# Four ordering edges in a one-core transformer block: two on VectorE and two normalisations on ScalarE

## The chip, the cores and the metric

The kernel runs on one NeuronCore of a Trainium2 chip. The metric is device time in microseconds (us) of one execution. PE is TensorE, DVE is VectorE, ACT is ScalarE, SP is the engine that issues most of the DMAs (307 of 325 in the kernel before). The profile's span (first to last instruction) is about 1.8 us shorter than the timed value of the same execution. Each execution also comes with a mean granted TensorE clock, 1.000 being full speed.

## The reference, cut to what matters

```python
phi = lambda t: jnp.where(t > 0, t + 1, jnp.exp(t)) + 1e-6
q, k, v = split(layernorm(x) @ wqkv)                    # S = 2048, D = 1024, 32 heads of 32
kv = einsum("bhsd,bhse->bhde", phi(k), v);  z = sum over s of phi(k)
o = (phi(q) @ kv) / (phi(q) . z + 1e-6)
h = x + o @ wo
h2 = h + ((relu(hn @ W_gate)) * (hn @ W_up)) @ W_down   # hn = layernorm(h), F = 3584
```

## The kernel before

Every large product is one level of Strassen-like block products: seven products in place of eight, with sums of operand blocks made beforehand on VectorE and partial results copied out of PSUM, the memory that TensorE adds its products up in, between the products; to copy a PSUM bank out is to evict it (0.68 us for one of 128x512 on VectorE in the second K unit). Three stages matter here.

*K units.* Each takes four token tiles; the first of the four units is computed plainly, the others start near 39, 67 and 95 us. (This text counts them from one; the prediction counts from zero, so its K unit 1 is the second here.) In the last three `strassen` accumulates products in the PSUM banks A, D and E. ScalarE copies the accumulators out (`snap`), VectorE evicts D and E (`phi_begin`), and both also normalise x for later units or make operand sums for the next product.

```python
def right_ops(w, t):                        # operand sums of a weight, on VectorE
    def sums():
        tensor_tensor(out=t1, in0=b12, in1=b11, op=subtract)
        tensor_tensor(out=t2, in0=b22, in1=t1, op=subtract)
        tensor_tensor(out=t3, in0=b22, in1=b12, op=subtract)   # in the place of b12
        tensor_tensor(out=t4, in0=b21, in1=t2, op=subtract)

def phi_begin(dst, ps, m):                  # evicts a PSUM bank
    if m is None: nc.scalar.activation(out=dst, in_=ps[:], func=Identity, bias=..., scale=1.0)
    else:         nc.vector.scalar_tensor_tensor(out=dst, in0=ps[:], scalar=1.0 + PHI_EPS, in1=m, ...)

def phi_end(dst, e):
    nc.scalar.activation(out=e, in_=dst, func=Exp, ...)
    nc.vector.tensor_scalar(out=e, in0=e, scalar1=1.0, scalar2=PHI_EPS, op0=min, op1=add)   # "the clip"
    nc.vector.tensor_tensor(out=dst, in0=dst, in1=e, op=max)
```

*The attention tail (200 to 232 us).* For each token tile: `nd` matmuls (numerator and denominator), the division on VectorE (`o_sb`), a DMA transpose, 16 `attn` matmuls with wo, an addition of the residual on VectorE (`x_res`), a normalisation on ScalarE (`hn`), and a DMA transpose of `hn`.

*The first quad of the gated layer* starts in the middle of that. Its operands are sums of the transposed `hn` and of the gate and up weights, all on VectorE:

```python
def left_sums(T, S, cols, eng):             # for each token tile of the second half of a group
    eng.tensor_tensor(out=s1, in0=a21, in1=a22, op=add)        # "hs", reads the transposed hn
    eng.tensor_tensor(out=s2, in0=s1, in1=a11, op=subtract)
    eng.tensor_tensor(out=a21, in0=a11, in1=a21, op=subtract)
    eng.tensor_tensor(out=s4, in0=a12, in1=s2, op=subtract)
...                                          # then weight sums: "tg", "tu"
```

A list scheduler decides the order of the instructions on each engine from a model of their durations. An edge "behind" orders two instructions of one engine and adds no wait; but everything else on that engine, and on others, may then be placed anew.

## Time and profile before

| | kernel before |
|---|---|
| time, first 6 runs | 738.26 us median (737.57 to 739.62) |
| time, 33 runs beside the experiments | 738.47 us median, 738.68 mean |
| span of the profiled run | 737.2 us, clock 1.000 |
| PE busy | 98% of the span |

PE is the bound; the gain to be had is in the 14.5 us that it idles (737.2 - 722.7). A line of the order of time reads: start, duration, engine, source line, operation, output<-input, shapes, count, and in brackets the idle time before it and what ended that. Source lines shift by up to a dozen between the kernels (`o_sb` is L534 before and L544 after); go by the tile names.

### The profile page before, as it was taken

The page shows a single profiled execution, that of the slowest core. Times are in us where ns is not written, and L with a number is a line of the kernel's source. Part 1 is how long each engine was busy: PE and PEld are TensorE (multiplying, and loading weights), DVE is VectorE, ACT ScalarE, POOL GpSimd, SP SyncE. Part 2 cuts the span into 40 slices and gives each one's busy share as a digit, 9 for nine tenths or more (in the row PEclk, how much of TensorE's full clock was granted, in tenths as well). Part 3 has the DMA queues.
Part 4 walks back from the last instruction along what each step waited for, and adds up shares of the span by engine and source line. Part 5 has one row for each costly group of instructions (what it writes and reads, how often), then busy time and mean ns, then how long its engine had stood idle before and what let it go on. Part 6 is the DMA issues. An engine that isn't in the chain of part 4 may idle for free.

```text
span 737.2 us, 10549 instructions
## 1 busy us (share of the span) xinstructions
PE 722.7 (98%) x3967; PEld 381.8 (52%) x4020; DVE 556.0 (75%) x980; ACT 321.5 (44%) x580; POOL 20.7 (3%) x56
## 2 busy tenths in 40 slices
PE   8999999999989999999999999999999999999997
PEld 3444555444444444444444444444444458888667
DVE  6997644676789767688768787887786479996677
ACT  4776553778786655444344444443444120000000
POOL 0000000000000000000000000000000001100210
PEclk9999999999999999999999999999999999999999
DMA  9765002079977526175638358575483499978932
GB/s 315 169 145 157 0 1 95 21 168 230 215 166 166 135 73 208 43 207 135 196 106 243 114 188 270 182 219 193 162 280 120 137 392 343 305 253 283 257 44 58
DMA packets 143811, 128.88 MB, mean 175 GB/s; under 512 B 50960, under 2 KB 126096, under 8 KB 143760
## 3 DMA queue, kind: packets, MB, share of 16 engines
q1 hardware_dynamic: 136688, 123.30, 55.6%
q0 software_dynamic: 5312, 3.15, 3.4%
q10 hardware_dynamic: 1760, 1.77, 0.7%
q8 instruction: 31, 0.51, 0.3%
q14 instruction: 20, 0.16, 0.1%
HBM read 76.81 MB, written 39.85 MB: 158 GB/s over the span
## 4 chain that ended last, share of the span: by engine, by line
PE 85%; DVE 7%; DMA 4%; ACT 3%; issue 1%; SPq 0%; DVEq 0%; POOL 0%; ACTq 0%
PE accA L832 22%; PE accX L832 8%; PE accY L832 8%; PE accA L1167 8%; PE attn L557 6%; PE Aq L733 4%; PE Aq L314 3%; PE accA L993 3%; PE accX L1167 3%; PE Aq L454 3%; PE accY L1167 2%; PE Eq L314 2%; PE accY L993 2%; PE accX L993 2%; PE Eq L733 2%; DVE stats L272 1%
## 5 line engine op out<-in xcount | busy, mean ns | idle before, releaser
L842 ACT ACTIVATE gu<-gu 128x512 bf16<-128x512 bf16 x72 | 45.4, 630 | 131.3 <-DVE gu L841 131.3
L837 ACT COPY snap<-accA 128x1024 f32<-128x1024 f32 x72 | 72.5, 1008 | 36.5 <-PE accA L832 36.4
L832 PEld LDWEIGHTS <-tg 128*128 128x128 f16 x384 | 37.6, 98 | 45.3
L832 PEld LDWEIGHTS <-tu 128*128 128x128 f16 x384 | 37.6, 98 | 45.3
L557 PE MATMUL attn<-wo_mem,oT 128*128 128x512 bf16 x247 | 57.9, 379 | 2.6 <-DVE o_sb L534 1.3
L841 DVE TENSOR_TENSOR gu<-accY,snap 128x1024 bf16<-128x1024 f32 x36 | 43.9, 1219 | 10.0 <-ACT snap L837 10.0
L832 PE MATMUL accA<-hn,tg 128*128 128x512 f16 (+1 forms) x192 | 49.3, 379 | 0.0
L832 PE MATMUL accA<-hn,tu 128*128 128x512 f16 (+1 forms) x192 | 49.3, 379 | 0.0
L841 DVE TENSOR_TENSOR gu<-accX,snap 128x1024 bf16<-128x1024 f32 x36 | 43.9, 1219 | 6.4 <-PE accX L832 3.7
L154 ACT COPY u<-Aq 128x512 f32<-128x512 f32 x54 | 31.3, 581 | 36.6 <-PE Aq L314 19.3
L1167 PEld LDWEIGHTS <-x 128*128 128x128 f16 (+1 forms) x448 | 43.9, 98 | 5.5
L832 PEld LDWEIGHTS <-wu 128*128 128x128 bf16 x288 | 28.2, 98 | 34.0
L832 PEld LDWEIGHTS <-wg 128*128 128x128 bf16 x288 | 28.2, 98 | 34.0
L557 PEld LDWEIGHTS <-oT 128*128 128x128 bf16 x256 | 24.6, 98 | 32.5 <-issue 4.1
L845 DVE TENSOR_TENSOR hq<-gu 128x512 bf16<-128x512 bf16 x48 | 20.3, 423 | 14.3 <-ACT gu L842 14.2
L314 PEld LDWEIGHTS <-xT 128*128 128x128 bf16 (+1 forms) x192 | 18.6, 98 | 23.6 <-issue 2.3
L534 DVE TENSOR_TENSOR o_sb<-nd,rd 128x384 bf16<-128x384 f32 (+1 forms) x48 | 23.4, 508 | 8.3 <-ACT rd L533 6.1
L1131 POOL DMA_DIRECT2D out_dram<-o x12 | 15.2, 1265 | 508.8 <-DMA h<-h_dram 419.1
L1167 PEld LDWEIGHTS <-xs 128*128 128x128 f16 x280 | 27.4, 98 | 3.2
L560 DVE SCALAR_TENSOR_TENSOR x_res<-attn,x_res 128x512 bf16<-128x512 f32 x32 | 22.0, 686 | 8.6 <-PE attn L557 8.5
L1173 DVE TENSOR_TENSOR snap<-accA,u 128x1024 f32<-128x1024 f32 x16 | 19.5, 1221 | 11.4 <-PE accA L1167 11.3
L993 PEld LDWEIGHTS <-x 128*128 128x128 bf16 (+1 forms) x168 | 16.4, 98 | 19.6
(235 smaller groups left out, 1420.3 us busy)
## 6 DMA issues: line engine op xcount, KB each, us to landing
x<-x_dram SPq DMA_DIRECT2D x17, 896.0 KB, 8.8
x_dram<-hq SPq DMA_DIRECT2D x28, 512.0 KB, 3.2
wg<-in_B_W_gate_dram SPq DMA_DIRECT2D x14, 512.0 KB, 5.1
wu<-in_B_W_up_dram SPq DMA_DIRECT2D x14, 512.0 KB, 7.3
wraw<-in_B_W_down_dram SPq DMA_DIRECT2D x14, 512.0 KB, 4.9
x_dram<-hq SPq DMA_DIRECT2D x28, 256.0 KB, 2.7
t_dram<-wt SPq DMA_DIRECT2D x28, 256.0 KB, 2.2
xd<-x_dram SPq DMA_DIRECT2D x6, 896.0 KB, 6.9
```

The source lines that it names most:

```text
L154: copies[nm, v] = nc.scalar.copy(out=snaps[nm, v], in_=bank[v][:])
L314: nc.tensor.matmul(ps[:], lhsT=left[m - 1][:, kc, r + v * P:r + (v + 1) * P], rhs=right[m - 1][:, kc, :], start=(start and kc == 0), stop= ...
L454: nc.tensor.matmul(ps[:], lhsT=rq[m - 1][:, kc, (c + v) * P:(c + v + 1) * P], rhs=left[m - 1][:, kc, :], start=(start and kc == 0), stop=( ...
L534: nc.vector.tensor_tensor(out=ov[:, c0:c0 + n], in0=ndv[:, :, 0:P].rearrange("p k (h e) -> p k h e", h=HPC), in1=rd[:, 0:n, :].unsqueeze(3 ...
L557: nc.tensor.matmul(ps[:], lhsT=st["oT"][:, c, :], rhs=wo_sb[:, c, j * NW:(j + 1) * NW], start=(c == 0), stop=(c == KC - 1))
L733: nc.tensor.matmul(ps[:], lhsT=w(v, m)[:, kc, :], rhs=left[m - 1][:, kc, :], start=(start and kc == 0), stop=(kc == KH - 1), skip_group_ch ...
L832: nc.tensor.matmul(ps[:, v, :], lhsT=w[v][n - 1][:, kc, :], rhs=left[n - 1][:, kc, :], start=(t is not None and kc == 0), stop=(kc == KH - ...
L837: nc.scalar.copy(out=st[nm][:], in_=halves(st["A"]))
L841: add(out=g[:], in0=halves(st[nm]), in1=st[base][:], op=ALU.add)
L842: nc.scalar.activation(out=g[:, 0, :], in_=g[:, 0, :], func=ACT.Relu)
L993: nc.tensor.matmul(ps[:, t * NW:(t + 1) * NW], lhsT=x_tile(n, s, kh)[:, f, (t0 + t) * P:(t0 + t + 1) * P], rhs=w_tile(n, kh)[:, f, :], sta ...
L1167: nc.tensor.matmul(pv[:, tt, :], lhsT=left(m)[:, f, tt * P:(tt + 1) * P], rhs=right(m)[:, f, :], start=(t is not None and f == 0 and tt % ...
```

## The change

The intent is to take away five short waits of PE, by order alone. Part A: two normalisations of x go behind accumulator copies of the second K unit on ScalarE. Part B: the second q sum goes behind the first D eviction of the fourth and last K unit, near 97 us, and so no longer stands ahead of the third's. Part C: the last clip of the q side goes behind the `x_res` addition of a tile. No arithmetic changes.

```diff
+    def behind(late, first):
+        tc.add_manual_dep(late.ins, first.ins.name, <order only, same engine>)
+    normed, k_copies, k_begins, q_ends = {}, {}, {}, {}
 ...   (the instructions concerned are kept in these dictionaries)
-        q_sums()
+        behind(q_sums(), k_begins[NU - 1, 0, 0, 0])                              # part B
+        for t, copy in ((atiles[10], ("m1", 1)), (atiles[11], ("u3", 0))):
+            behind(normed[t], k_copies[1][copy])                                 # part A
 ...
     with tc.issue_after(added[order[STS], 0].ins):
         late_sums.pop()()
+    behind(q_ends[NS - 1, KH - 2, 1, 0], added[order[STS], 0])                   # part C
```

(`q_sums()` returns its second instruction; two older edges were only rewritten with `behind`. So the new edges are four.)

More of the change, by code (lines that the diff above doesn't have):

```diff
@@ L133, in sums @@
             nc.vector.tensor_tensor(out=t1, in0=b12, in1=b11, op=ALU.subtract)
-            nc.vector.tensor_tensor(out=t2, in0=b22, in1=t1, op=ALU.subtract)
+            second = nc.vector.tensor_tensor(out=t2, in0=b22, in1=t1, op=ALU.subtract)
             nc.vector.tensor_tensor(out=t3, in0=b22, in1=b12, op=ALU.subtract)
             nc.vector.tensor_tensor(out=t4, in0=b21, in1=t2, op=ALU.subtract)
+            return second
         return (b11, b21, b22, t4, t1, t2, t3), sums
@@ L208, in phi_begin @@
         if m is None:
-            nc.scalar.activation(out=dst, in_=ps[:], func=ACT.Identity, bias=negb[:, 1:2], scale=1.0)
-        else:
-            nc.vector.scalar_tensor_tensor(out=dst, in0=ps[:], scalar=1.0 + PHI_EPS, in1=m,
-                                           op0=ALU.add, op1=ALU.add)
+            return nc.scalar.activation(out=dst, in_=ps[:], func=ACT.Identity, bias=negb[:, 1:2], scale=1.0)
+        return nc.vector.scalar_tensor_tensor(out=dst, in0=ps[:], scalar=1.0 + PHI_EPS, in1=m,
+                                              op0=ALU.add, op1=ALU.add)
     def phi_end(dst, e):
         nc.scalar.activation(out=e, in_=dst, func=ACT.Exp, bias=negb[:, 0:1], scale=1.0)
-        nc.vector.tensor_scalar(out=e, in0=e, scalar1=1.0, scalar2=PHI_EPS, op0=ALU.min, op1=ALU.add)
+        clipped = nc.vector.tensor_scalar(out=e, in0=e, scalar1=1.0, scalar2=PHI_EPS, op0=ALU.min, op1=ALU.add)
         nc.vector.tensor_tensor(out=dst, in0=dst, in1=e, op=ALU.max)
+        return clipped
+    def behind(late, first):
+        tc.add_manual_dep(late.ins, first.ins.name,
+                          mybir.DependencyInfo(mybir.DependencyClass.NoSync, mybir.DependencyReason.DATA),
+                          reason="order")
+    normed, k_copies, k_begins, q_ends = {}, {}, {}, {}
     order = [(i * HS + s * SW) // P + tt for s in range(NS) for i in range(2) for tt in range(NT)]
@@ L287, in ln_T @@
             nc.vector.scalar_tensor_tensor(out=nmr, in0=mv[:, 0:1], scalar=-1.0, in1=rstd, op0=ALU.mult, op1=ALU.mult)
-            nc.scalar.activation(out=xn[:], in_=x_sb[:], func=ACT.Identity, bias=nmr, scale=rstd)
+            normed[t] = nc.scalar.activation(out=xn[:], in_=x_sb[:], func=ACT.Identity, bias=nmr, scale=rstd)
             if t not in atiles[:PE_T]:
@@ L305, in block_kernel, with token_unit @@
         pk, vs = {}, {}
-        def token_unit(u, right, fin):
+        def token_unit(u, right, fin, copies={}):
             s, _, r = place(units[u][0])
@@ L316, in mm @@
                                      stop=(kc == KH - 1), skip_group_check=True)
-            return strassen(pspool, awork, mm, fin)
+            return strassen(pspool, awork, mm, fin, 3, False, copies)
         def new_pk(t):
@@ L330, in fin @@
                     new_pk(t)
-                phi_begin(pk[t][:, j * NW:(j + 1) * NW], ps, m)
+                k_begins[u, i, j, v] = phi_begin(pk[t][:, j * NW:(j + 1) * NW], ps, m)
                 ready[t] = ready.get(t, 0) + 1
@@ L335, in fin @@
                     phi_end(pk[t], e[:])
-            return token_unit(u, rk, fin)
+            return token_unit(u, rk, fin, k_copies.setdefault(u, {}))
         def k_plain(t):
@@ L462, in fin @@
                 e = qw[-1].tile([P, 2, NW], BF16, tag="e", name="e")
-                phi_end(pair, e[:])
+                q_ends[s, c, i, j] = phi_end(pair, e[:])
         return strassen(pspool, qw[-1], mm, fin, 3, s == NS - 1 and c + 2 == KH)
@@ L790, in block_kernel @@
     for t, copy in ((order[-2], ("m1", 1)), (order[-1], ("u3", 1))):
-        tc.add_manual_dep(squared[t].ins, quad_copies[2][copy].ins.name,
-                          mybir.DependencyInfo(mybir.DependencyClass.NoSync, mybir.DependencyReason.DATA),
-                          reason="order")
+        behind(squared[t], quad_copies[2][copy])
     pqctx.close()
```

## The prediction

> **What bounds the kernel now.** I read the page's busy shares first, then PE's waits, then the order of time around each wait. PE is busy almost throughout:
>
> ```profile
> PE 722.7 (98%) x3967; PEld 381.8 (52%) x4020; DVE 556.0 (75%) x980; ACT 321.5 (44%) x580; POOL 20.7 (3%) x56
> ```
>
> The span is 737.2 us, so PE idles 14.5 us. Busy time by stretches puts 2.9 of it in the first 10 us, 3.7 after PE's last matmul, 1.7 between 39 and 82, 2.0 between 200 and 232, and 4.2 in all the rest. Nothing that moves work on DVE (VectorE) or ACT (ScalarE) can win more than the few waits in between. PE's waits name the ones that the change aims at:
>
> ```profile
> PE attn L557 <- DVE x_res L560: 0.8, 1, 0.8
> PE nd L527 <- DVE o_sb L534: 0.5, 1, 0.5
> PE Dq L314 <- DVE wo_mem L211: 0.5, 1, 0.5
> PE Aq L314 <- ACT m L154: 0.5, 1, 0.5
> PE Aq L314 <- ACT u L154: 0.3, 1, 0.3
> ```
>
> That view counts from a matmul's modelled end. I count from where the next could have started: eight 512-column matmuls take 1.73 us from start to start, so 0.216 each, and a 132-column one 0.058. By that the waits in the order of time, in their order here, are 0.98, 0.64, 0.64, 0.62 and 0.44 us. Outside these two stretches PE runs nearly without gaps and nothing is waiting to absorb a shift: what is lost or won at these places reaches the end undiminished.
>
> The order of time around the first two, DVE, PE and the DMA queue together:
>
> ```profile
> 210.93 0.43 DVE L217 TENSOR_SCALAR e<-e 128x1024 bf16<-128x1024 bf16 x1 [0.94 <-ACT e L216]
> 211.28 0.69 DVE L560 SCALAR_TENSOR_TENSOR x_res<-attn,x_res 128x512 bf16<-128x512 f32 x1
> ...
> 212.02 0.59 PE L557 MATMUL attn<-wo_mem,oT 128*128 128x512 bf16 x2 [0.82 <-DVE x_res L560]
> ...
> 213.02 1.23 SPq L581 DMA_TRANSPOSE hn<-hn  x1
> ...
> 216.07 0.96 DVE L534 TENSOR_TENSOR o_sb<-nd,rd 128x384 bf16<-128x384 f32 x2
> 216.94 0.68 DVE L560 SCALAR_TENSOR_TENSOR x_res<-attn,x_res 128x512 bf16<-128x512 f32 x1
> ...
> 217.55 0.42 DVE L117 TENSOR_TENSOR hs<-hn 128x512 f16<-128x512 bf16 x1
> ```
>
> The reader is to see three things. At 210.93 DVE had idled 0.94 us for an exponential while the x_res addition behind it was ready. The hn transpose is issued at 213.02. The first sum that reads it, hs on L117, runs at 217.55 without a wait, because two o_sb and one x_res stand ahead of it.
>
> The transpose of hn in that stretch, alone:
>
> ```profile
> DMA to landing us min/median/max: 4.4/4.4/4.4
> ```
>
> It lands at 213.02 + 4.4 = 217.42, just before L117 wants it. (For the transpose at 200.90 the view gives 4.0, and its reader starts at 204.97 after a DMA wait: the count runs from the start of the issue.)
>
> [...]x_res at 211.28 has its operands from 209.5 and comes after the 0.94 us wait. [...]The trace has 1.24, so that is what one blocks a copy for. [...]the transposes here take 3.0 to 6.0, and the trace is what I use.
>
> **The change part by part.** It adds and removes no arithmetic: five order-only edges move instructions. Comparing the built programs, the instructions of DVE, ACT and PE are reordered in two regions (39 to 99 us, 211 to 228 us), and the DMA queue's order is the same.
>
> Part A, two normalisations on ACT. Those of tiles 10 and 11 go behind the second m1 copy and the first u3 copy of K unit 1. The second m1 copy then runs at about 41.4 instead of 43.12, and the 0.62 wait at 43.11 goes. But the next D matmul waits for DVE anyway:
>
> ```profile
> 42.99 1.22 DVE L136 TENSOR_TENSOR tv<-wv_sb,tv 128x2048 f16<-128x2048 bf16 x1
> 44.12 0.68 DVE L211 SCALAR_TENSOR_TENSOR wo_mem<-Dq,m 128x512 bf16<-128x512 f32 x1
> 44.86 0.81 PE L314 MATMUL Dq<-pq_mem,xT 128*128 128x512 bf16 x3
> ```
>
> DVE is busy without a break from 36.9 to that eviction, and in the new order the same work stands ahead of it. So D still starts at 44.86: gain 0. At 49.3 the wait on a u3 copy (0.44) goes too, but the new DVE order puts four statistics (0.6 each) and their small ones ahead of the first E eviction, which starts at about 49.97; PE, which now takes E there, waits until 50.7, 0.5 us. Net -0.1 to 0. The pushed normalisations (2 x 1.14 us from start to start) then stand among the exponentials and copies of the V unit; walking ACT, DVE and PE in the new order I get waits of 0.2, 0.2 and 0.35 to 0.5 us there, about 0.7 in all lost by the start of K unit 2. This walk is the least certain: 0 to 0.9.
>
> Part B, the q sums. The second and fourth (1.22 us each) move from ahead of K unit 2's D eviction to behind the last unit's first D eviction. The 0.64 wait at 71.6 goes. In their new place they end near 99.8, the next eviction ends near 100.4, and the V unit wants that D bank only near 110: free. Gain 0.64.
>
> Parts A and B together: 0.7 lost, 0.64 won, about 0.1 slower.
>
> Part C, the clip (e, L217) behind the x_res addition. x_res can start at 209.92 instead of 211.28, so the wait on it goes. PE's order changes with it: the nd group now stands where the two attention matmuls stood. nd needs the o_sb eviction, whose reciprocal ACT delivers at 211.44; DVE does it at about 211.5 to 212.05. So PE waits from 211.04 to 212.05: 1.0 in place of 0.98. The second wait (0.64) shrinks to about 0.05, and PE is some 0.6 ahead at 216.0.
>
> Here the bill comes. In the new DVE order hs L117 of that tile stands two o_sb and one x_res earlier. DVE reaches it at about 215.3, and the transpose lands at 217.42; ACT and the DMA queue ahead of it are unchanged, so it lands no sooner. DVE stands 2.1 us with both o_sb behind it: L117 217.45, o_sb 217.8 and 218.3 (0.34 and 0.48 from start to start). The second nd group, which PE reaches at 216.2, needs the PSUM bank of the first of these and starts at 218.3: 2.1 us lost. Then DVE still owes o_sb, x_res, three more hs sums and the row sum (0.4 + 0.6 + 3 x 0.34 + 0.12) before the first weight sum tg, which formerly ran at 214.95 and is now behind them: tg starts near 220.4 and ends 220.8. PE has its E matmul ready at 219.5 and waits 1.3 more; before, the wait for tg there was 0.58. Counting matmuls to the start of the next attention group: 223.7 with 17 of 18 done, against 221.83 with 18 done, so 1.9 + 0.2 = 2.1 us slower.
>
> Sum: 0.1 + 2.1 = 2.2 us slower. I take 0.3 off, since the wait at 249.2 (0.56) may absorb a little: 737.7 + 1.9 = 739.6 us.
>
> **The rivals.** First: the edges do what they are meant to. All aimed-at waits go and nothing comes in their place: 0.98 + 0.64 + 0.64 + 0.62 + 0.44 = 3.3 us, 734.4. Against it speak the tv sums at 42.99 and the unchanged landing at 217.42; for it, that somebody placed the edges at measured waits. Second: the transpose lands earlier [...]near 3.5 us after issue (216.5). Then DVE stands 1.2 us, region C costs about 1.2 instead of 2.1, and the total is near 738.8. Third: the V unit's waits do not come (my ACT walk is too slow), A and B give 0.6, and the total is 739.0; with the second rival too, 738.1. Fourth: DVE falls so far behind that later quads wait as well, 741.
>
> **Range and chances.** The mechanism of part C rests on one landing time and a fixed order, so I give slower than before about four in five. From the combinations above, 737.0 to 740.9 should hold it 8 times in 10; below lies the first rival in part. Two per cent would be 14.8 us, as much as PE's whole idle time: faster 0.004, within 2% 0.99, slower 0.006.
>
> **What would show it.** Right: in the changed kernel DVE waits about 2 us for DMA hn before hs L117 near 215 to 217; PE nd waits about 2 us for o_sb there, then PE waits about 1.3 us on tg; the x_res wait of attn is gone; the Dq wait near 72 is gone; the D matmul of K unit 1 still starts near 44.9. PE's busy time stays near 722.7. Wrong: no DMA wait at hs L117 (the transpose was earlier, or DVE later); no new waits in the V unit from 55 to 67; or a gain at 44.86, which would mean that DVE's sums were not what D waited for. If the total falls below 736.5, part C's bill is wrong.

(The 1.24 us is one normalisation on ScalarE, `xn<-x_sb`, 128x1024: 1.24 us in the mean of 15 in the kernel before. That a DVE instruction that waits holds up what stands behind it is read from the rows at 210.93 and 211.28. The second rival's 3.5 us is an estimate; the transposes in that profile took 3.0 to 6.0.)

## More of the kernel before

One view that the prediction did not use is needed later: busy time by stretches. Its columns are the stretch, its length, then busy us and count for PE, its weight loads, DVE, ACT and POOL, then the granted clock, the DMA share and GB/s. For the kernel before, around the start of the quad:

```profile
219.00:220.00 1.00, 0.59 (x4) 0.27 (x4) 1.00 (x4) 1.00 (x6) 0.00 (x0) 1.00 1.14 301
220.00:221.00 1.00, 1.00 (x6) 0.25 (x4) 1.00 (x4) 0.97 (x4) 0.00 (x0) 1.00 0.70 143
```

The clock column (third from the end) is 1.00 in both.

## The result, and the profile after

The changed kernel took 742.01 us in the median of 6 runs (740.35 to 744.12), against 738.26 for the kernel before in the same rounds. The ratio is 1.0053, 95% interval 1.0034 to 1.0071. Ratios here are the mean of one kernel's fast runs over the mean of the other's of the same rounds, so not quite the ratio of the medians. It is the same at the 2% mark, slower beyond doubt, and outside the predicted range (737.0 to 740.9). On another chip, later, the same kernel took 740.14 against 738.47. That the two sittings differ so much is part of the puzzle.

PE's waits of the changed kernel (waiter, what it waited for, us in total, times, longest):

```profile
PE nd L537 <- DVE o_sb L544: 1.9, 2, 1.7
PE Dq L322 <- DVE wo_mem L211: 1.6, 2, 0.8
PE Eq L743 <- DVE tg L650: 1.1, 1, 1.1
```

The waits for `x_res` and for ScalarE's copies `m` and `u` are gone; others are in their place. The order of time where most of it is lost, SP's queue, DVE and PE together:

```profile
212.44 2.23 SPq L591 DMA_TRANSPOSE hn<-hn  x1
...
216.51 0.43 DVE L117 TENSOR_TENSOR hs<-hn 128x512 f16<-128x512 bf16 x1 [1.88 <-DMA hn<-hn]
216.86 0.88 DVE L544 TENSOR_TENSOR o_sb<-nd,rd 128x384 bf16<-128x384 f32 x2
...
217.46 0.33 PE L537 MATMUL nd<-kvz,pq_mem 128*128 128x132 bf16 x3 [1.72 <-DVE o_sb L544]
...
219.87 1.46 PE L743 MATMUL Eq<-hs,tg 128*128 128x512 f16 x3 [1.09 <-DVE tg L650]
...
221.12 1.91 PE L743 MATMUL Aq<-hs,tg 128*128 128x512 f16 x4
```

DVE stands 1.88 us at the head of its queue for the transposed `hn`; the `o_sb` behind it is late, so PE stands 1.72; the weight sum `tg`, which formerly ran before, is late too, so PE stands 1.09 more. All this was predicted. Now look at the last two rows. Three Eq matmuls take 1.25 us from start to start, 0.42 each, where 0.216 is usual. The busy times by stretches of the changed kernel say why:

```profile
219.00:220.00 1.00, 0.14 (x1) 0.13 (x2) 1.00 (x4) 1.00 (x3) 0.00 (x0) 0.77 1.12 211
220.00:221.00 1.00, 1.00 (x3) 0.30 (x2) 1.00 (x4) 0.97 (x8) 0.00 (x0) 0.50 1.32 323
221.00:222.00 1.00, 1.00 (x4) 0.33 (x3) 1.00 (x4) 1.00 (x1) 0.00 (x0) 0.50 0.45 158
222.00:223.00 1.00, 1.00 (x4) 0.43 (x3) 1.00 (x3) 0.17 (x1) 0.00 (x0) 0.53 1.19 306
```

PE counts as fully busy from 220 on, but at half clock, and does 3 to 4 matmuls per us where the kernel before did 6. Half clock lasts 0.46 + 1 + 1 + 0.94 = 3.40 us (each term is twice what the slice lacks to 1.00). Matmuls were in flight for some 3.1 us of it, so about 1.5 us went here.

The next `attn` group starts at 224.18 with 17 matmuls of the quad done since the `nd` group; before, it started at 221.83 with 18 done. From there to the end the two take 515.62 and 515.37 us, and one matmul still owed accounts for 0.2 of the difference. So nothing is lost or won back later, and the 0.3 us that the prediction took off for that is not there.

The first stage did little. In the third K unit of the changed kernel:

```profile
69.43 1.23 DVE L133 TENSOR_TENSOR tq<-wq_sb 128x2048 f16<-128x2048 bf16 x1 [1.26 <-DMA wq_sb<-in_A_wqkv_dram]
...
70.69 1.23 DVE L135 TENSOR_TENSOR wq_sb<-wq_sb 128x2048 f16<-128x2048 bf16 x1
...
71.84 0.68 DVE L211 SCALAR_TENSOR_TENSOR wo_mem<-Dq,m 128x512 bf16<-128x512 f32 x1
...
72.57 1.02 PE L322 MATMUL Dq<-pq_mem,xT 128*128 128x512 bf16 x4 [0.82 <-DVE wo_mem L211]
```

The second q sum (line 134) has left, but the first and the third now stand ahead of the eviction, and the first waits for its weight. In the second K unit D still starts late, at 44.57, 0.79 behind the eviction.

The mean clock of a run hints at whether there was half clock in it: one stretch of 3.4 us, as above, lowers the mean of a 738 us span by 1.7/738 = 0.0023, two by 0.0046. The six runs of the changed kernel had 0.997, 0.997, 1.000, 0.995, 0.997, 0.995, and in spans 739.8, 740.3, 738.6, 742.4, 740.2, 741.4 us. The one at full clock is the fastest. (0.999 need not mean a loss: in the profile of experiment 12 below, at 0.999, the clock is 1.00 in every stretch up to 602 us; in that of the kernel before it falls only at 736.73 us, after PE's last matmul, which ends at 733.49.)

### The profile page after: what moved, and what is told of

It is laid out like the page before. It is cut to its first block, busy times and chain, and to the rows that moved or that the text cites. A ratio compares the mean times of both kernels' runs of the same rounds, so it can differ in the third digit from the quotient of the medians.

```text
span 739.8 us, 10607 instructions
## 1 busy us (share of the span) xinstructions
PE 725.4 (98%) x4020; PEld 382.3 (52%) x4020; DVE 556.6 (75%) x980; ACT 322.0 (44%) x580; POOL 21.0 (3%) x56
## 4 chain that ended last, share of the span: by engine, by line
PE 81%; DVE 8%; ACT 5%; DMA 4%; issue 1%; SPq 0%; DVEq 0%
PE accA L841 22%; PE accY L841 8%; PE accX L841 8%; PE accA L1176 8%; PE attn L567 4%; PE Aq L322 4%; PE accA L1002 3%; PE accX L1176 3%; PE Aq L464 3%; PE Aq L743 3%; PE accY L1176 2%; PE Eq L322 2%; PE accX L1002 2%; PE accY L1002 2%; DVE stats L280 2%; PE Eq L743 2%
## 5 line engine op out<-in xcount | busy, mean ns | idle before, releaser
L322 PEld LDWEIGHTS <-xT 128*128 128x128 bf16 (+1 forms) x192 | 18.7, 98 | 24.3 <-issue 2.9
L1002 PEld LDWEIGHTS <-x 128*128 128x128 bf16 (+1 forms) x168 | 16.5, 98 | 19.6
```

The source lines that it names most:

```text
L322: nc.tensor.matmul(ps[:], lhsT=left[m - 1][:, kc, r + v * P:r + (v + 1) * P], rhs=right[m - 1][:, kc, :], start=(start and kc == 0), stop= ...
L1002: nc.tensor.matmul(ps[:, t * NW:(t + 1) * NW], lhsT=x_tile(n, s, kh)[:, f, (t0 + t) * P:(t0 + t + 1) * P], rhs=w_tile(n, kh)[:, f, :], sta ...
```

## The experiments

The theory: the clip edge lets DVE stand for `hn`, PE then idles twice close together, and these idles cost twice: as waits, in every run, and by the halved clock, in some. Rivals: the other two parts cost something of their own; or the clock falls for another reason than idling. Each kernel below ran 5 or 6 times, beside the kernel before on the same chip; all results were correct.

**1. The clip edge alone.**

```diff
-        behind(q_sums(), k_begins[NU - 1, 0, 0, 0])
+        q_sums()
-        for t, copy in ...: behind(normed[t], k_copies[1][copy])
```

> Only the clip edge, nothing of the two other parts. Theory 1 (the clip edge makes VectorE stand at the head of its queue for the hn transpose, TensorE then idles 1.72 and 1.09 us close together, and the granted clock falls to about half for some 3 us after it): nearly the whole loss of the full change is here, 740.5 to 742.5 us, with the wait of 1.9 us of VectorE for hn near 216 to 217 us of the span and a mean clock of 0.995 to 0.997 in most runs. Rival (the loss comes from all three parts together, or from the V unit's late copies): 738 to 739.5 us here.

Measured: 739.85 us, ratio 1.0018 (1.0006 to 1.0031); clocks 1.000, 1.000, 0.999, 0.997, 0.998. It is slower than the kernel before, but by 1.3 us in the median, not by 2 to 4. The profiled run, at clock 1.000, has the two idles in full:

```profile
216.79 0.34 PE L535 MATMUL nd<-kvz,pq_mem 128*128 128x132 bf16 x3 [1.79 <-DVE o_sb L542]
...
219.20 0.82 PE L741 MATMUL Eq<-hs,tg 128*128 128x512 f16 x3 [1.09 <-DVE tg L648]
```

Here the Eq matmuls take their usual time. So the waits do not bring the half clock with them in every run, and this single run could not say whether A and B cost the rest.

**2. Parts A and B without the clip edge.** The edit leaves out the line of part C.

> The two other parts without the clip edge. Theory 1: no wait of VectorE for hn, no idle of 1.7 us on TensorE near 217 us, clock 1.000, 738.0 to 738.7 us, that is 0 to +0.3 us against the kernel before. Rival (these parts carry some of the loss): 739.5 us or more. The wait of 0.8 us for the wo_mem eviction near 72 us should still be there, since the third q sum stands ahead of that eviction.

Measured: 738.51 us, ratio 1.0001 (0.9987 to 1.0014); clocks 0.999, 1.000, 1.000, 1.000, 0.998. Nothing lost, nothing won. The rival that these parts carry some of the loss by themselves falls.

**3. The full change, mended.** The hs sum that reads the transposed `hn` is ordered behind the `o_sb` that PE waits for.

```diff
+    behind(hn_sums[STS - 1], evicted[order[STS + 3], 2 * GPB])
```

> The full change plus one ordering edge: the first hs sum of the last tile of the first token half stands behind the o_sb eviction that TensorE waits for. Theory 1: VectorE's wait for hn is 0 to 0.5 us, TensorE has no idle over 0.8 us between 212 and 222 us, the clock is 1.000, and what the clip edge gained (the wait of about 0.9 us for x_res near 212 us) stays: 737.3 to 738.4 us, 0 to 0.9 us under the kernel before. Rival (the head-of-queue wait is not the cause): stays near 742 us.

Measured: 738.52 us, ratio 0.9997 (0.9984 to 1.0009); all six runs at clock 0.999 or 1.000. With the head-of-queue wait taken away, waits and half clock go together:

```profile
215.60 0.42 DVE L117 TENSOR_TENSOR hs<-hn 128x512 f16<-128x512 bf16 x1
...
217.54 1.04 PE L745 MATMUL Aq<-hs,tg 128*128 128x512 f16 x4 [0.45 <-DVE tg L656]
```

The expected gain below the kernel before (737.3 to 738.4) is not seen, although in the profiled run the stretch from the quad's first matmul (204.85) to the next `attn` group (219.88) is 15.0 us, against 15.6 to 16.5 in four traces with the clip in its old place (the kernel before, experiment 2 and the two single parts below). One trace each is too little against a spread of about 1 us either way between runs of any kernel here.

**4. The idles filled.** The full change; TensorE's two idle stretches are filled with matmuls whose results are overwritten.

```diff
         def mm(ps, m, v, start):
+            if (fc, v) == (0, 0) and m in (2, 5):
+                dummies[m] = [matmul(ps[:], lhsT=ident[:], rhs=wo_sb[:, 0, 0:NW], start=True, stop=True)
+                              for _ in range({2: 8, 5: 5}[m])]
+    (edges that put them ahead of the waiting nd and Eq matmuls)
```

> The full change with its waits left as they are, but TensorE's two idle stretches filled with matmuls whose results are thrown away (8 before the nd matmul that waits for o_sb, 5 before the first Eq matmul that waits for tg), in the order of the changed kernel. If the halved clock follows from TensorE's idling (theory 1): clock 1.000 in nearly every run, no slice at half clock near 219 to 223 us, 739.0 to 740.3 us, 1.7 to 3 us under the changed kernel although it does 13 matmuls more and VectorE waits as long. Rival (the clock falls for another reason, or the loss is all waiting): 741.5 to 743 us.

Measured: 742.12 us, ratio 1.0053 (1.0037 to 1.0069); clocks 0.998, 0.999, 1.000, 1.000, 1.000, 1.000. The clock held, as expected; the time did not fall, against the expectation. The scheduler had moved later work, with new waits (0.9 us at one attn group, 0.6 at an accumulator). The one run with 0.998 is the profiled one, and its half clock is not at 219 us but near the start, after a wait of 2.0 us that PE has there for its first transposes:

```profile
10.00:11.00 1.00, 1.00 (x5) 0.31 (x3) 0.14 (x2) 0.95 (x1) 0.00 (x0) 0.50 1.05 378
```

The traces of all kernels have a wait of 1.6 to 2.9 us there, so such a stretch is a candidate for the rare low clocks of kernels without the two idles.

**5. The full change again, and 6. the clip edge again**, on one chip.

> The changed kernel itself, once more, as the control of this chip. Its clock was 0.995 to 0.997 in five of six runs. Expected: again below 0.999 in most of its runs, 740.5 to 743 us.

> The clip edge alone, a second time, on the same chip as the full change. It has the same two idles of TensorE (1.79 and 1.09 us), 0.7 us earlier. If the clock's fall is drawn run by run from where the idle lies: some runs at 1.000, some at 0.997, 739.3 to 741.3 us, and the fast ones of the full change (clock 1.000) are within 0.8 us of the fast ones of this. Rival (the other two parts cost 2 us of their own beside the clip edge): the full change is slower at equal clock, by about 2 us.

Measured: the full change 740.14 us, ratio 1.0030 (1.0015 to 1.0045), clocks 1.000, 1.000, 0.998, 0.997, 0.999, 1.000; it was below 0.999 in two of six runs, not in most. The clip edge alone 740.40 us, ratio 1.0031 (1.0016 to 1.0047), clocks 1.000, 0.999, 0.995, 1.000, 0.997, 0.998. On one chip the two are equal: the other two parts cost nothing beside the clip edge either. The difference between the first sitting of the full change and experiment 1 lay mostly in how many runs had the low clock (5 of 6 against 2 of 5). What decides that for a run is taken up after the table below.

**7. The idles filled, with every engine's order pinned** to the order of the changed kernel, so that only the 13 matmuls differ (and the ordering edges themselves; the pinned order without these matmuls was not run).

```diff
+    for eng, runs in ORDER.items():          # the changed kernel's own order, engine by engine
+        seq = [made[eng][a + k] for a, c in runs for k in range(c)]
+        (8 dummies ahead of the nd matmul, 5 ahead of the first Eq matmul)
+        for p, q in zip(seq, seq[1:]): behind(q, p)
```

> The first filling of the idle let the scheduler move later work, which brought new waits (0.9, 0.6 us and smaller ones) after the place in question. Here every engine's order is pinned to the order of the changed kernel, and the only difference is the 8 and 5 matmuls with thrown-away results in TensorE's two idle stretches. If the half clock follows from that idling: clock 0.999 or 1.000 in nearly every run, and 739.5 to 740.8 us, 1.5 us or more under the changed kernel of the same chip. Rival (the loss is the wait, the clock falls anyway): the time of the changed kernel, and clocks of 0.995 to 0.997.

Measured: 741.55 us, ratio 1.0042 (1.0029 to 1.0055); clocks 1.000, 1.000, 1.000, 0.999, 1.000. The same stretch of the profiled run:

```profile
219.00:220.00 1.00, 1.00 (x7) 0.39 (x4) 1.00 (x5) 0.71 (x1) 0.00 (x0) 1.00 0.62 122
220.00:221.00 1.00, 0.99 (x6) 0.22 (x4) 1.00 (x4) 1.00 (x7) 0.00 (x0) 1.00 1.15 278
```

The clock part of the theory passes: the waiting of DVE is as it was, only PE's idling is gone, and no run fell. The time again misses the expectation: the stretch from the quad's first matmul to the next `attn` group takes 17.0 us (18.7 in the changed kernel's first profile, with the half clock, and 16.8 in its second, at full clock), but the run is about 1.5 us longer after 224 us, in small waits near 266, 279, 551 and 614 us, each of which shifts the matmuls behind it by 0.3 to 0.4 us against the second profile of the changed kernel. Why matmuls that fill an idle bring these is open, so the times of the filled kernels say nothing about the size of the clock's share; their clocks do point to idling as its cause: 2 of 23 runs at 0.998 or below in the four kernels with filled idles, against 12 of 23 with both idles.

**8. and 9. One idle filled at a time,** in the pinned order: the first (8 matmuls), or the second (5).

> Pinned order of the changed kernel, with only the first and longer idle of TensorE (1.6 to 1.8 us) filled; the second (1.1 us) stays. If the half clock needs both idles close together: clock 0.999 or 1.000 in nearly every run, as where both were filled. If the second alone is enough: clocks of 0.998 and less in about half the runs.

> Pinned order of the changed kernel, with only the second idle of TensorE (1.1 us) filled; the first (1.6 to 1.8 us) stays. If the first alone is enough for the half clock: clocks of 0.998 and less in about half the runs, 12 of 23 in the kernels with both idles so far. If it takes both: 0.999 or 1.000 in nearly every run.

Measured, first filled: 741.14 us, ratio 1.0038 (1.0026 to 1.0051), clocks 0.999, 1.000, 1.000, 0.999, 1.000, 0.999. Second filled: 740.71 us, ratio 1.0035 (1.0021 to 1.0048), clocks 0.999, 1.000, 1.000, 0.998, 1.000, 1.000. The idle that stays, in each of the two:

```profile
219.89 0.82 PE L56 MATMUL Eq<-hs,tg 128*128 128x512 f16 x3 [1.09 <-DVE tg L56]
```

```profile
217.68 0.33 PE L56 MATMUL nd<-kvz,pq_mem 128*128 128x132 bf16 x3 [1.61 <-DVE o_sb L56]
```

Neither alone brought the clock down as both do, though these are six runs each, on a chip where no kernel with both idles ran; the traces below are in keeping with that. (With the pinned order all lines are that of a helper.)

**10. Part A alone, and 11. part B alone.** (In the texts of experiments 11 and 12, the edge behind the "third" K unit's eviction is behind the fourth's, as in the change itself; the wait aimed at is the third's.)

> Only the two normalisations behind the accumulator copies of the second K unit. Reading so far: VectorE, not ScalarE, still ends the wait near 44 us, and the V unit that follows gets one or two waits of 0.2 to 0.3 us. Expected: equal to the kernel before within 0.5 us, the waits of TensorE on ScalarE's m and u copies near 44 and 50 us gone, a wait of 0.8 to 0.9 us on the wo_mem eviction near 44 us in their place. Rival (the normalisations were the bound there): 0.7 us or more under it.

> Only the second q sum behind the eviction of the third K unit's first D. The prediction on record says the wait of 0.47 to 0.8 us near 72 us goes. The reading since then: the first and the third sum still stand ahead of that eviction, and the first waits for the weight's load. Expected now: the wait near 72 us is still there with 0.2 to 0.8 us, and the time is equal to the kernel before within 0.5 us; rival (it was the transfer's later landing in the full change that spoilt it): the wait is gone and the time 0.5 us lower.

Measured: part A 738.65 us, ratio 1.0004 (0.9992 to 1.0016); part B 738.26 us, ratio 0.9999 (0.9987 to 1.0011). In part A's trace the waits on ScalarE's copies are gone and one of 0.88 us on the DVE eviction stands at 44.59, as read. In part B's trace:

```profile
70.34 1.22 DVE L135 TENSOR_TENSOR wq_sb<-wq_sb 128x2048 f16<-128x2048 bf16 x1
71.48 0.68 DVE L211 SCALAR_TENSOR_TENSOR wo_mem<-Dq,m 128x512 bf16<-128x512 f32 x1
```

The weight landed by 67.40 here, 2 us earlier than in the full change, and still D waits 0.50 us at 72.21, because the third sum stands directly ahead of the eviction. So it is the order, and the later landing only adds to it. That landing is part A's doing: the weight's loads are issued at 60.2 and 61.6 us in the full change, in experiment 2 and with part A alone, and at 59.1 to 61.3 in the kernel before and with part B alone; with part A alone D waits 0.79 us at 72.56, against 0.47 before.

**12. A version meant to beat both:** the mended one, with the first q sum in the place of the second, behind the eviction of the fourth K unit, and also the third V sum behind the eviction of the second K unit.

```diff
-        behind(q_sums(), k_begins[NU - 1, 0, 0, 0])
+        behind(q_sums()[0], k_begins[NU - 1, 0, 0, 0])
-                v_sums()
+                behind(v_sums()[2], k_begins[1, 0, 0, 0])
```

> The mended version (hs sum behind the o_sb eviction) and, beside it, the first instead of the second q sum ordered behind the eviction of the third K unit, and the third V sum behind the eviction of the second K unit, so that neither stands ahead of the eviction that TensorE waits for. If the reason why the q edge gained nothing is that the first and third sums still stand ahead of the eviction: the waits of 0.4 to 0.8 us near 72 us and of 0.9 us near 44 us are gone, and the time is 736.5 to 738.0 us, 0.5 to 1.8 us under the kernel before. Rival (those waits are followed by others): equal to the kernel before within 0.5 us.

Measured: 738.18 us, ratio 0.9998 (0.9986 to 1.0010). The waits aimed at shrank (0.33 us at 44.54, 0.40 at 72.67), and one grew:

```profile
50.83 0.59 PE L323 MATMUL Eq<-pq_mem,xS 128*128 128x512 bf16 x2 [0.89 <-DVE wo_mem L212]
```

There it was 0.35 in part A's trace. The rival holds: DVE is full in that stretch (no gap in this trace from 40.95 to 52.65 us), and what is moved off one eviction lands before another. No version here beats the kernel before measurably.

**All runs by clock.** "Both idles" are the changed kernel and the clip edge alone, two sittings each.

| group | runs | runs at 0.998 or below | mean time at 0.999 and above | mean time below |
|---|---|---|---|---|
| both idles | 23 | 12 | 739.83 us | 742.12 us |
| one or both idles filled (4, 7, 8, 9) | 23 | 2 | not comparable | |
| kernel before, 33 runs | 33 | 3 | 738.51 us | 740.42 us |
| 2, 3, 10, 11, 12 | 26 | 1 | 738.44 us | one run, 739.36 us |

So the clip edge costs 739.83 - 738.51 = 1.3 us at full clock, and a further 742.12 - 739.83 = 2.3 us in about half of the runs. The full change over its 12 runs averages 741.50, against 738.68: 2.8 us slower.

**What decides it for a run.** The profiles give part of an answer. Each keeps records of the granted clock. In the changed kernel's first profile there is one of full clock from 4.49 to 219.53 us, one of half clock to 222.95, one of full clock to 738.36, and half clock from there on, after PE's last matmul, which ends at 736.08. The half clock lasts 3.413 us, and the two at full clock 215.04 and 515.41 us, which is 63 and 151 times 3.413 to within 0.1. In the kernel before, the one record of full clock lasts 730.45 us, from 6.28 to 736.73: 214 times 3.413. So both traces can be cut into stretches of 3.413 us with every change of the clock at a cut, and the cuts do not lie at the same places of the two spans. First the two stretches at whose end the clock fell, in the changed kernel's first profile and in experiment 4's (the other traces here were cut in the same way):

```profile
216.12:219.53 3.41, 1.31 (x9) 0.58 (x8) 3.02 (x10) 2.14 (x5) 0.00 (x0) 1.00 0.74 157
6.59:10.01 3.41, 1.42 (x13) 0.88 (x12) 1.94 (x5) 0.41 (x2) 0.00 (x0) 1.00 1.09 359
```

Then two at whose end it stayed, in the changed kernel's second profile and in experiment 12's:

```profile
214.96:218.37 3.41, 1.63 (x13) 0.78 (x11) 2.48 (x8) 2.26 (x8) 0.00 (x0) 1.00 0.75 181
7.59:11.00 3.41, 1.52 (x10) 0.80 (x10) 2.26 (x6) 1.57 (x4) 0.00 (x0) 1.00 1.08 365
```

PE idled 2.10 and 1.99 us in the first two, 1.78 and 1.89 in the others. The profiles of the kernel before and the changed kernel's first have 428 such stretches at full clock: the three with the most idle (2.10 us, and 2.28 and 3.24 at the end, where the matmuls run out) were followed by half clock, none of the other 425, with 1.66 us or less. The length of an idle does not tell it alone: in experiment 12's profile PE waits 2.92 us up to 9.48, a wait that the cut at 7.59 divides, and the clock stays at 1.00. From this the reading is that the idle within one stretch decides; no experiment moved the cuts, so it is not shown. One idle of the pair alone (at most 1.79 us) is less than any sum that half clock followed here; both are 2.8 us within 4.1, and by this reading it depends on where the cuts divide them. An estimate from the changed kernel's first profile, with the cuts moved over it: a stretch with 2 us or more in about a quarter of the positions. The 12 of 23 runs are more than that; the wait at the start may add some (3 of 33 runs of the kernel before), and whether the rest is chance is not shown.

## Why the prediction was wrong, point by point

- **Part C, the mechanism of the waits, right.** DVE standing at hs L117 for the `hn` transpose, PE's `nd` waiting for `o_sb`, then the wait on `tg`, and the `x_res` wait gone: all seen. Experiments 1 and 3 show the cause by giving the loss and taking it away.
- **Part C, the missing term, which took the result out of the range.** The step "2.1 us slower" counted waits only and took every matmul at 0.216 us. The granted clock was not in the sum. After the two idles it was 0.50 for 3.40 us in the first profile, 0.42 us a matmul, about 1.5 us there. Over all runs the low clock goes with 2.3 us in 12 of 23 of them (a mean of 0.995 is as much as two such stretches). None of the four rivals had it. The first idle and the second had been predicted at 2.1 and 1.3 us, together more than the 2.10 us of idle that came before the half clock, so the idle for it was in the working. The changed kernel's five runs at full clock average 740.0 us, inside the range, its seven others 742.6. Why the first sitting had five of the latter in six is not shown.
- **Part C, the landing, wrong.** The step "ACT and the DMA queue ahead of it are unchanged, so it lands no sooner" failed. The normalisation of `hn` started at 210.8 instead of 211.4, the transpose was issued at 212.44 instead of 213.02, and it took 4.1 instead of 4.4 us: 216.51 instead of 217.42. (The transposes of `hn` between 195 and 230 us took 3.3 to 4.4 us in the two profiles, 3.0 to 6.0 over the whole kernel.) The edge is not the reason: the DVE sum that waits for an earlier `hn` transpose, ahead of all that moved, already runs at 204.38 instead of 204.97. From the quad's first matmul to that normalisation it is 5.3 us here and in experiment 2, where the clip stands in its old place, and 6.1 in the one profile that the prediction read. By the same 0.6 us the `o_sb` of the first `nd` group was ready sooner: the 1.0 us forecast for PE there was 0.18. With the earlier landing the waits came to 1.72 and 1.09 rather than 2.1 and 1.3, and the bill at full clock to 1.3 rather than 2.1 us. That is the second rival, which was given its own number (1.2) but not the centre.
- **Part C, the aimed-at wait.** The 0.98 for `x_res` was that of the one profiled run of before. In the traces of experiments 2, 10 and 11, which have the same order there, no wait on `x_res` is listed. The gain that part C could bring was smaller than that profile suggested.
- **Part B, wrong.** "The 0.64 wait goes" failed. The third sum, 1.23 us, stands ahead of the eviction once the second has left, and the first waits for its weight; the step counted neither. Experiment 11 has the third sum in that place with the weight early.
- **Part A, gain 0, right.** D of the second K unit is still bound by DVE (44.57 in the full change, 44.59 alone). The waits in the V unit came, 0.17 and 0.31 us, smaller than the 0.7 walked; from the start of the second K unit to that of the third it is 27.98 us against 27.85, so about 0.1 is lost.
- **The base.** The prediction stood on the first three runs (737.7); in the six of the result the kernel before had 738.26, over 33 later ones 738.47. That is 0.6 to 0.8 us of the 2.4 us between prediction and result.

## What to carry to other kernels

An edge that only orders one instruction moves others, and a DVE instruction that waits for a DMA can then come to stand ahead of evictions that PE needs: after adding an edge, look at what now stands behind every DMA reader. When PE's idles come close together, add them up (here 2.10 us within 3.41 came before half clock, though a single wait of 2.92 us in experiment 12 did not bring it), and look at the granted clock after them, slice by slice, and at the clock of every run: the same waits cost a further 2.3 us here in about half of the runs and nothing in the others. And where an engine is full (DVE, busy for all of 38 to 54 us in the kernel before), an order that takes one wait away makes another; a trace of one run each cannot show gains of half a microsecond when runs spread by 1.
